# Four-batch products of v_m and w1: two heads side by side on the row halves of the array, three terms of 64 rows each

## The chip, the core and the metric

The kernel runs on one core of a Trainium2 chip. The metric is the time of one execution on the device in microseconds (us); several executions are timed and the median counts, and one execution is recorded by the profiler. The engines are called PE (the matrix engine; PEld is its loading of weights), DVE (VectorE), ACT (ScalarE), POOL (GpSimd) and SP (SyncE, which here only issues transfers).

## The reference

Eight batches of eight heads with 576 rows of 64 pass through an attention over 32 memories per head, and the result through four experts.

```python
a = softmax(phi)                                  # b h s m
k_m = np.einsum('bhsm,bhsd->bhmd', a, k)
v_m = np.einsum('bhsm,bhsd->bhmd', a, v)
attn = softmax(scale * np.matmul(q, k_m.transpose(0, 1, 3, 2)))
x = np.matmul(attn, v_m)                          # 4608 x 512 once the heads are joined
for e in range(E):                                # 4 experts
    h = np.maximum(x @ w1[e], 0.0)                # w1: 512 x 1024
    out += p[:, e:e + 1] * (h @ w2[e])            # w2: 1024 x 512
```

## The kernel before

**Precision.** A factor stands as a high part rounded to float32r and a low part, the remainder, and a product is made of terms: high by high, high by low, low by high.

**What is multiplied.** `x` is never formed. The kernel multiplies v_m by w1 first and attn by that: `h = relu(attn @ (v_m @ w1))`. `v_m @ w1` for a batch, an expert and a half `fh` of the 1024 columns is a tile `vw`. It is made in one of two ways. `vw_mm` (lines 539 to 545) does it for two heads and two batches at a time. `four_mm` does it for one head and four batches at a time (4 x 32 memories fill the 128 columns of weights). The second way serves expert 3 of the batches 0 to 3 and all experts of the batches 4 to 7, in all 5 pairs of expert and batch group, times two halves, times eight heads: 80 products.

**How a four-batch product is laid.** `write_v` (434 to 450) puts v_m of four batches into the tile `vs`: the 64 partitions 0 to 63 hold the high part of a head, the partitions 64 to 127 its low part. The 64 rows of w1 that belong to the head come doubled over both halves from an input `w1d` made for this. So two matmuls of 128 rows and 512 columns give all four terms, with the high part of w1 (`w[:, 0]`) and then with the low (`w[:, 1]`).

**Its steps.** `units_four` (601 to 618) makes the work of a pair `hp` of heads. A load takes a staged 512 KB tile of `w1d`; `four_split` makes the high part on ACT (line 163) and the low part on POOL (line 164), once for each of the two heads; `four_mm` fills a PSUM bank; `four_out` (590 to 595) copies it out, the high part on ACT (592) and the low part on DVE (593), and gives the bank back; `to_memory` (572 to 576) has POOL store the result, to be loaded by `load_vw`.

**What sets the order.** From step 36 on the order is written by hand: `plan[s]` holds what is issued in step s, in the order of the calls of `at`. Up to step 191 (`BEGIN` is 192) a step is a `first` (attn by vw, lines 649 to 651) and a `second` (h by w2, lines 682 to 684), with four banks of the pool "pm" between `first`, the products and the attention. From there on `unit(u)` runs, four steps long, with products by `product` (line 1019), `rows` (933 to 935) and, in every fourth unit, `middle` (1057 to 1059). In it "pm" has two banks, for the four-batch products, for `middle` and for the attention (scores, line 463, and transposes, line 521). Banks go round in turn: `bank` takes the one that was given back first, and an instruction that writes a bank waits for the last one that read it. 16 of the 80 products lie before step 192, 64 in units.

A unit issues on PE, in this order: `run_plan(s)`, six matmuls "a11", six `rows`, `run_plan(s + 1)` behind which `middle` stands, "a12", six `rows`, "t2", `run_plan(s + 2)`, "t3", six `rows`, "t1", `run_plan(s + 3)`, "n4", six `rows`, "a22". `add_in` (1037, DVE) adds each result to the accumulator. `x_relu` (967, ACT) and `x_out` (975, 976, 979 and in part 947 and 948) prepare the next unit. DVE, ACT and POOL each work their instructions in order, so an instruction that `run_plan` puts in stands behind all that the unit has issued there.

With the profile's line numbers:

Of the kernel before, what the change touches and what calls it, by code (L numbers as in the profile page):

```python
# [9 lines left out]
F32 = mybir.dt.float32  # L10
F32R = mybir.dt.float32r
# [17 lines left out]
PAIR = E * STEPS  # L29
# [9 lines left out]
FOUR = (3, 0)  # L39

FOUR_AT = ((6, 8, 10, 13), (15, 17, 20, 22))
FOUR_LAG = 2


W2_AT = (20, 23, 25, 27)
# [7 lines left out]
ATT = {  # L53
    2: (22, 30, 48, (92, 96, 101), (111, 112, 113)),
    3: (38, 46, 65, (116, 118, 120), (PAIR + 2, PAIR + 4, PAIR + 6)),
    4: (88, 96, 114, (PAIR + 75, PAIR + 79, PAIR + 91), (PAIR + 99, PAIR + 103, PAIR + 107)),
    5: (107, PAIR - 2, PAIR + 16, (PAIR + 111, PAIR + 115, PAIR + 123), (PAIR + 119, PAIR + 125, PAIR + 131)),
    6: (PAIR + 3, PAIR + 14, PAIR + 32, (2 * PAIR + 23, 2 * PAIR + 27, 2 * PAIR + 35), (2 * PAIR + 31, 2 * PAIR + 33, 2 * PAIR + 43)),
    7: (PAIR + 18, PAIR + 32, PAIR + 50, (2 * PAIR + 98, 2 * PAIR + 102, 2 * PAIR + 106), (2 * PAIR + 115, 2 * PAIR + 116, 2 * PAIR + 117)),
}  # L60

# [7 lines left out]
BEGIN = SEVEN[0] * PAIR + SEVEN[1] * STEPS  # L69
# [9 lines left out]
FOUR_AT_7 = ((0, 4, 8, 12), (16, 20, 24, 28))  # L79
# [3 lines left out]


@with_exitstack
def body(ctx: ExitStack, tc: tile.TileContext, qm, qt, kv, kvt, phi, prob, w1, w1d, w2, out):
    nc = tc.nc
    pool = lambda name, **k: ctx.enter_context(tc.tile_pool(name=name, bufs=1, **k))
    const, wp, work, att = pool("const"), pool("wp"), pool("work"), pool("att")
# [5 lines left out]
    def bank(tag, *shape):  # L95
        n = idle[tag].popleft()
        out = banks[:, n, :]
        m = 1
        for d in shape:
            m *= d  # L100
        names = "abcd"[:len(shape)]
        out = out[:, :m].rearrange(
            f"p ({' '.join(names)}) -> p {' '.join(names)}", **dict(zip(names, shape))
        )
        lent[id(out)] = tag, n, out
        return out

    def give(ps):
        tag, n, _ = lent.pop(id(ps))
        idle[tag].append(n)  # L110
# [12 lines left out]

    def source(key):
        kind, *i = key
        return {"kv": kv, "kvt": kvt, "qm": qm, "qt": qt, "w1": w1, "w1d": w1d, "w2": w2}[kind][tuple(i)]

    order, staged, count, spare = [], {}, [0, 0], []

# [32 lines left out]
    def split(dst, raw, eng):  # L162
        nc.scalar.copy(dst[:, 0, :], raw)  # L163
        eng.tensor_sub(dst[:, 1, :], raw, dst[:, 0, :].bitcast(F32))  # L164
# [6 lines left out]
    def unit_w1(k, e, fh, g):  # L171
        def emit(raw):
            for i in range(2):
                split_w1(raw, fh, 2 * g + i, nc.vector)
        return ("w1", e, fh, g), emit
# [79 lines left out]
    st = {}  # L255
# [157 lines left out]
    def slot(b, h):  # L413
        return h ^ TURN[b % 4]
# [19 lines left out]
    def write_v(b, pair):  # L434


        if b % 4 == 0:
            st["vs", b // 4] = att.tile([P, 2, 4, P], F32R, name="vs", tag="vs")
        vs = st["vs", b // 4]
        vt = vts[b // 2].rearrange("p (g a) s c -> p g a s c", g=2) if pair else None  # L440
        v = st["vh", b].rearrange("p s (g a) m -> p s g a m", g=2)
        for h in range(4):
            q = slot(b, h)
            rq, c = slice(64 * (q % 2), 64 * (q % 2) + 64), slice(M * q, M * q + M)
            rh = slice(64 * (h % 2), 64 * (h % 2) + 64)
            for i in range(2):
                src = v[rq, i, :, q // 2, :].bitcast(F32)
                nc.sync.dma_start(vs[64 * i:64 * i + 64, :, h, c].bitcast(F32), src)
                if pair:
                    nc.sync.dma_start(vt[rh, :, h // 2, i, c].bitcast(F32), src)  # L450

    def tiles(t0):
        return (2, P) if t0 < 4 else (1, 64)
# [118 lines left out]
    def to_memory():  # L572
        for key, t in done:
            vwd[key] = dram.tile([P, 2, 512], F32, name="vwd" + "".join(map(str, key)))
            nc.gpsimd.dma_start(vwd[key], t.bitcast(F32))
        done.clear()

    def four_split(raw, i):
        w = wp.tile([P, 2, 512], F32R, name="w1", tag="w1", bufs=4)
        split(w, raw[:, i, :], nc.gpsimd)  # L580
        return w

    def four_mm(n, h, w):
        g, vs = h // 4, st["vs", n]
        ps = bank("pm", 512)
        for a in range(2):
            nc.tensor.matmul(ps, vs[:, g, h % 4, :], w[:, a, :], start=a == 0, stop=a == 1)  # L587
        return ps

    def four_out(n, e, fh, h, ps):  # L590
        t = att.tile([P, 2, 512], F32R, name="vst", tag="kvs", bufs=KVS)
        nc.scalar.copy(t[:, 0, :], ps)
        nc.vector.tensor_sub(t[:, 1, :], ps, t[:, 0, :].bitcast(F32))
        give(ps)
        done.append(((n, e, fh, h // 4, h % 4), t))

    def four(n, e, fh, h, w):
        to_memory()
        four_out(n, e, fh, h, four_mm(n, h, w))

    def units_four(n, e, fh, hp, gap=1):

        kept = {}
        def load(raw):
            kept["raw"] = raw
            kept[0] = four_split(raw, 0)
        def other():
            kept[1] = four_split(kept["raw"], 1)
        out = [(0, (("w1d", e, fh, hp), load)), (gap, other)]
        for i in range(2):  # L610
            h, x = 2 * hp + i, FOUR_LAG + gap * i
            if gap == 1:
                out.append((x, lambda i=i, h=h: four(n, e, fh, h, kept[i])))
                continue
            out.append((x, lambda i=i, h=h: kept.update({2 + i: four_mm(n, h, kept[i])})))
            out.append((x + 1, lambda i=i, h=h: four_out(n, e, fh, h, kept[2 + i])))
            out.append((x + 2, to_memory))
        return out

    def load_vw(k, e, odd, fh):  # L620
        b = 2 * k + odd
# [90 lines left out]
    def at(s, unit):  # L712
        plan[s].append(unit if isinstance(unit, tuple) else (None, unit))
# [80 lines left out]
    for k in range(NG):  # L794
        for e in range(E):
            s = k * PAIR + e * STEPS
            nk, ne = (k, e + 1) if e + 1 < E else (k + 1, 0)
            if nk == NG:
                continue
            by_four = ne >= FOUR[nk // 2]  # L800
            if s == 0:
                for j2 in range(4):
                    at(s + W2_AT[j2], unit_w2(nk, ne, j2))
                for fh in range(2):
                    for g in range(2):
                        at(s + W1_AT[2 * fh + g], unit_w1(nk, ne, fh, g))
                        for i in range(2):
                            vw_at(s + VW_AT + 4 * fh + 2 * g + i, nk, ne, fh, 2 * g + i, (0, 1))
                continue
            for j2 in range(4 if nk == 0 else 0):  # L810
                for i, u in enumerate(units_w2(nk, ne, j2)):
                    at(s + W2_FROM + 2 * j2 + i, u)
            for j in range(NJ if nk and s + STEPS < BEGIN else 0):
                at(s + W2_AGAIN + j, lambda a=(nk, ne, j): load_w2(*a))
            for fh in range(2):
                when, gap = (FOUR_AT_7, 2) if s >= BEGIN else (FOUR_AT, 1)
                for hp in range(NP if by_four and nk % 2 == 0 else 0):
                    for i, u in units_four(nk // 2, ne, fh, hp, gap):
                        at(s + when[fh][hp] + i, u)
                if by_four and nk % 2 == 0 and gap == 1:  # L820
                    at(s + when[fh][NP - 1] + FOUR_LAG + 2, to_memory)
                for odd in range(2 if by_four else 0):
                    when = VW_LOAD_AT if s < BEGIN else VW_LOAD_7
                    at(s + when[odd][fh], lambda a=(nk, ne, odd, fh): load_vw(*a))
                for g in range(0 if by_four else 2):
                    last = s + STEPS == BEGIN
                    when = (LAST_PAIR_AT if last else PAIR_AT)[fh]
                    for i, u in enumerate(units_w1(ne, fh, g)):
                        at(s + PAIR_W1[fh][2 * g + i], u)
                        gap = 1 if last and fh and g else 0  # L830
                        vw_steps(s + when[2 * g + i] + i * gap, gap, nk, ne, fh, 2 * g + i, (0, 1))
# [33 lines left out]
    for block in range(UNITS // 4):  # L865
        _, e, fh, _, _ = place_of(4 * block)
# [272 lines left out]
    with tc.manual_schedule():  # L1139
        raw = {key: take(later) for later, key in enumerate(early)}  # L1140
# [153 lines left out]
```

## Time and profile before

| what | value |
|---|---|
| median of 3 runs | 1377.34 us (1377.04 to 1381.64) |
| the profiled execution | 1377.26 us, of it 1375.5 us span |
| PE, DVE, ACT, POOL busy | 98%, 63%, 47%, 51% of the span |
| granted clock of PE | 0.998 |
| four-batch matmuls (line 587) | 160, from 257.2 to 1012.6 us |
| loads of `w1d` | 40 of 512 KB, 6.3 us to landing |

How it is read: PE records carry the start of an instruction; their ends are modelled, and matmuls overlap in the records. What a matmul costs in a stream is therefore the distance between the start of one and the start of the next, not its length. In a row of the timeline stand the start, the length, engine, line, operation, tiles, shape and count, and in brackets the idle time ahead of it.

### The profile page before, as it was taken

What the parts mean: (1) busy time and instruction counts of PE and PEld (TensorE: products, weight loads), DVE (VectorE), ACT (ScalarE), POOL (GpSimd) and SP (SyncE); (2) the same over time, 40 slices, a digit from 0 to 9 for tenths busy, and PEclk for the clock granted to TensorE, in tenths of its full rate; (3) what the DMA queues carried; (4) which work ended last, traced back from release to release, by engine and by line L of the source; (5) the groups of instructions that cost most, each with busy time, mean ns of one, the idle gap of its engine ahead of it and who ended that gap; (6) DMA issues with size and microseconds to landing.
All of it is one profiled execution on the core that took longest, in us unless ns stands there. A gap on an engine that the chain in (4) does not pass through costs nothing.

```text
span 1375.5 us, 26069 instructions
## 1 busy us (share of the span) xinstructions
PE 1353.9 (98%) x9182; PEld 1257.8 (91%) x9182; DVE 859.9 (63%) x1966; ACT 644.8 (47%) x1552; POOL 695.7 (51%) x743
## 2 busy tenths in 40 slices
PE   7899999999999999999999999999999999999998
PEld 6788888888888888889999999999999999999998
DVE  7875644445556445456677767767667666666665
ACT  6664565445535655453454544555543333333332
POOL 4300383648533626446866676677754334334432
PEclk9999999999999999999999999999999999999999
DMA  7652373898666454465789998999984866666661
GB/s 258 232 184 78 132 250 124 284 305 277 227 228 245 133 195 158 155 236 212 250 260 316 364 331 301 310 313 335 328 281 130 263 177 183 180 180 175 172 177 72
DMA packets 104338, 309.82 MB, mean 225 GB/s; under 512 B 25232, under 2 KB 26384, under 8 KB 104208
## 3 DMA queue, kind: packets, MB, share of 16 engines
q1 hardware_dynamic: 83472, 232.65, 53.6%
q0 software_dynamic: 19584, 71.31, 13.3%
q10 hardware_dynamic: 1152, 4.19, 0.8%
q8 instruction: 73, 1.20, 0.4%
q14 instruction: 57, 0.47, 0.1%
HBM read 221.85 MB, written 84.93 MB: 223 GB/s over the span
## 4 chain that ended last, share of the span: by engine, by line
PE 90%; DVE 4%; DMA 2%; ACT 1%; issue 1%; POOL 1%; SPq 0%; ACTq 0%; POOLq 0%; DVEq 0%
PE banks L1019 28%; PE banks L684 7%; PE banks L683 7%; PE banks L682 7%; PE banks L933 6%; PE banks L934 6%; PE banks L935 6%; PE banks L649 4%; PE banks L650 3%; PE banks L651 3%; PE banks L587 2%; PE banks L463 2%; PE banks L357 2%; PE banks L1057 1%; PE banks L1058 1%; PE banks L1059 1%
## 5 line engine op out<-in xcount | busy, mean ns | idle before, releaser
L1037 DVE SCALAR_TENSOR_TENSOR acc<-banks,pt,acc 128x256 f32<-128x256 f32 x528 | 253.0, 479 | 137.1 <-PE banks L1019 131.1
L164 POOL TENSOR_TENSOR w<-stage,w 128x512 fp32r<-128x512 f32 x134 | 173.8, 1298 | 149.0 <-ACT w L163 141.6
L1019 PE MATMUL banks<-w,a 128*128 128x256 f32 x1344 | 192.3, 282 | 0.3 <-DVE acc L1037 0.2
L933 PE MATMUL banks<-AT,vw 128*128 128x256 f32 (+1 forms) x640 | 189.5, 296 | 0.0
L934 PE MATMUL banks<-AT,vw 128*128 128x256 f32 (+1 forms) x640 | 188.9, 295 | 0.0
L935 PE MATMUL banks<-AT,vw 128*128 128x256 f32 (+1 forms) x640 | 188.8, 295 | 0.0
L1019 PEld LDWEIGHTS banks<-w,a 128*128 128x128 f32 x1344 | 179.2, 189 | 5.7 <-issue 0.6
L1000 POOL TENSOR_TENSOR vt<-ph,vt 128x512 fp32r<-128x512 f32 x80 | 103.8, 1297 | 108.2 <-ACT vt L999 71.8
L663 DVE SCALAR_TENSOR_TENSOR h<-banks,h 128x256 fp32r<-128x256 f32 x192 | 80.3, 420 | 124.0 <-ACT h L661 81.9
L684 PE MATMUL banks<-w,h 128*128 128x512 f32 x384 | 150.6, 393 | 2.2 <-DVE h L663 2.2
L682 PE MATMUL banks<-w,h 128*128 128x512 f32 x384 | 151.6, 395 | 0.1
L683 PE MATMUL banks<-w,h 128*128 128x512 f32 x384 | 151.1, 393 | 0.0
L661 ACT ACTIVATE h<-banks 128x256 fp32r<-128x256 f32 x192 | 73.4, 384 | 125.1 <-PE banks L651 99.6
L985 ACT ACTIVATE a<-banks 128x512 fp32r<-128x512 f32 x80 | 47.9, 598 | 166.1 <-DVE ph L991 131.1
L1010 POOL TENSOR_TENSOR tl<-xs,tl 128x256 fp32r<-128x256 f32 x80 | 59.3, 742 | 131.0 <-ACT tl L1009 72.2
L934 PEld LDWEIGHTS banks<-AT,vw 128*128 128x128 f32 x640 | 120.7, 189 | 0.1
L933 PEld LDWEIGHTS banks<-AT,vw 128*128 128x128 f32 x640 | 120.4, 188 | 0.4
L935 PEld LDWEIGHTS banks<-AT,vw 128*128 128x128 f32 x640 | 120.3, 188 | 0.0
L649 PE MATMUL banks<-AT,vw 128*128 128x320 f32 (+1 forms) x384 | 117.5, 307 | 1.3 <-DVE vw L563 0.9
L346 POOL TENSOR_TENSOR kvs<-stage,kvs 128x512 fp32r<-128x512 f32 x58 | 76.2, 1334 | 81.7 <-ACT kvs L345 73.7
L650 PE MATMUL banks<-AT,vw 128*128 128x320 f32 (+1 forms) x384 | 113.6, 296 | 0.0
L1019 PE MATMUL banks<-w,vt 128*128 128x256 f32 x768 | 112.6, 280 | 0.2 <-DVE acc L1037 0.2
(155 smaller groups left out, 3153.5 us busy)
## 6 DMA issues: line engine op xcount, KB each, us to landing
w<-kw SPq DMA_DIRECT2D x92, 512.0 KB, 5.7
vwd<-vst POOLq DMA_DIRECT2D x80, 512.0 KB, 6.5
vw<-vwd SPq DMA_DIRECT2D x320, 128.0 KB, 6.0
w<-v SPq DMA_DIRECT2D x68, 512.0 KB, 5.9
stage<-in_w SPq DMA_DIRECT2D x44, 512.0 KB, 4.4
stage<-in_w1d SPq DMA_DIRECT2D x40, 512.0 KB, 6.3
stage<-in_kv SPq DMA_DIRECT2D x32, 512.0 KB, 4.7
kw<-w POOLq DMA_DIRECT2D x24, 512.0 KB, 5.5
```

The source lines that it names most:

```text
L164: eng.tensor_sub(dst[:, 1, :], raw, dst[:, 0, :].bitcast(F32))
L649: nc.tensor.matmul(ps, w[:, 0, f], at_t[:, g, 0, c], start=g == 0, stop=False)
L650: nc.tensor.matmul(ps, w[:, 0, f], at_t[:, g, 1, c], start=False, stop=False)
L682: nc.tensor.matmul(po[t], x[:, 0, :], w[:, 0, :], start=j == 0, stop=False)
L683: nc.tensor.matmul(po[t], x[:, 0, :], w[:, 1, :], start=False, stop=False)
L684: nc.tensor.matmul(po[t], x[:, 1, :], w[:, 0, :], start=False, stop=j == NJ - 1)
L933: nc.tensor.matmul(ps, w[:, 0, f], at_t[:, g, 0, c], start=g == 0, stop=False)
L934: nc.tensor.matmul(ps, w[:, 0, f], at_t[:, g, 1, c], start=False, stop=False)
L935: nc.tensor.matmul(ps, w[:, 1, f], at_t[:, g, 0, c], start=False, stop=g == 1)
L1000: GP.tensor_sub(D[:, 1], d, D[:, 0].bitcast(F32))
L1019: nc.tensor.matmul(ps, a[:, l, jj], w[:, r, c], start=start and jj + i == 0, stop=jj == 1 and i == 2, skip_group_check=True,)
L1037: VE.scalar_tensor_tensor(a, src, p, a, ALU.mult, ALU.add)
```

## The change

Both heads of a pair are multiplied together. `vs` now has the layout of the tile that `vw_mm` uses: head 2hp on partitions 0 to 63, head 2hp + 1 on partitions 64 to 127, high and low part beside each other. A tile of w1 as it stands in the ordinary input `w1` has the rows of both heads on the same halves. So `w1d` goes, a load and a split serve two heads (20 loads and 40 splits instead of 40 and 80), and a pair takes six matmuls of 64 rows by 512 columns, alternating between the two halves and writing two banks, instead of four of 128 rows. The term low by low is left out.

The plan moves with it. In units, the second tile's split is now four steps behind the load; both heads are multiplied three steps behind their tile's split, always in `run_plan(s + 3)` of a unit, and take both banks; they are copied out in `run_plan(s)` and `run_plan(s + 1)` of the next unit. Before, the head products stood in `run_plan(s)` and `run_plan(s + 2)`, and were copied out one step later each. The attention's scores and transposes that fell on `run_plan(s + 3)` of these units are moved to `run_plan(s)`, where a bank is given back. Before step 192 both heads of a pair are multiplied in one step instead of in two, and copied out in that step and the next.

```diff
-FOUR_LAG = 2
+FOUR_LAG, FOUR_LAG_7 = (2, 2), (3, 4)
...
-    4: (88, 96, 114, (PAIR + 75, PAIR + 79, PAIR + 91), (PAIR + 99, PAIR + 103, PAIR + 107)),
...
+    4: (88, 96, 114, (PAIR + 75, PAIR + 79, PAIR + 91), (PAIR + 100, PAIR + 104, PAIR + 108)),
...
-            st["vs", b // 4] = att.tile([P, 2, 4, P], F32R, name="vs", tag="vs")
-        vs = st["vs", b // 4]
+            st["vs", b // 4] = att.tile([P, NP, 2, P], F32R, name="vs", tag="vs")
+        vs = st["vs", b // 4].rearrange("p (g a) s c -> p g a s c", g=2)
...
-                nc.sync.dma_start(vs[64 * i:64 * i + 64, :, h, c].bitcast(F32), src)
-                if pair:
-                    nc.sync.dma_start(vt[rh, :, h // 2, i, c].bitcast(F32), src)
+                for t in [vs] + [vt] * pair:
+                    nc.sync.dma_start(t[rh, :, h // 2, i, c].bitcast(F32), src)
...
-    def four_mm(n, h, w):
-        g, vs = h // 4, st["vs", n]
-        ps = bank("pm", 512)
-        for a in range(2):
-            nc.tensor.matmul(ps, vs[:, g, h % 4, :], w[:, a, :], start=a == 0, stop=a == 1)
+    def four_mm(n, hp, w):
+
+        vs, ps = st["vs", n], [bank("pm", 512) for _ in range(2)]
+        for t, (l, r) in enumerate(((0, 0), (0, 1), (1, 0))):
+            for i in range(2):
+                half = slice(64 * i, 64 * i + 64)
+                nc.tensor.matmul(
+                    ps[i], vs[half, hp, l, :], w[half, r, :], start=t == 0, stop=t == 2
+                )
         return ps
...
+    def units_four(n, e, fh, g, when, lag):
 
         kept = {}
         def load(raw):
             kept["raw"] = raw
+            kept["w", 0] = four_split(raw, 0)
+        def out(i, hp):
+            to_memory()
+            four_out(n, e, fh, 2 * hp + i, kept["ps", hp][i])
+        units = []
+        for a in range(2):
+            x, hp = when[2 * g + a], 2 * g + a
+            if a:
+                units.append((x, lambda: kept.update({("w", 1): four_split(kept["raw"], 1)})))
+            else:
+                units.append((x, (("w1", e, fh, g), load)))
+            units.append((x + lag[0], lambda a=a, hp=hp: kept.update({("ps", hp): four_mm(n, hp, kept["w", a])})))
+            for i in range(2):
+                units.append((x + lag[1] + i, lambda i=i, hp=hp: out(i, hp)))
+            units.append((x + lag[1] + 2, to_memory))
+        return units
```

Three places show the new order, all around the first transposes of batch 4 among the units. The first is PE in `run_plan(s + 3)`, between "t1" and "n4". Before (L1019 with `t_` is "t1", with `tl` "n4"; L521 are the transposes):

```order
L1019 MATMUL banks<-w_6160,t_7104 128x256 x2
L1019 MATMUL banks<-w_6281,t_7104 128x256 [waits DMAHW7_49]
L1019 MATMUL banks<-w_6281,t_7104 128x256 x2
L521 MATMUL banks<-ident,at 128x128 x4
L1019 MATMUL banks<-w_6257,tl 128x256 [waits DVE_49]
L1019 MATMUL banks<-w_6257,tl 128x256 x2
L1019 MATMUL banks<-w_6279,tl 128x256 x3
L933 MATMUL banks<-AT,vw 128x320
L934 MATMUL banks<-AT,vw 128x320
```

The same place with the change (L588 is the four-batch product):

```order
L1019 MATMUL banks<-w_6144,t_7088 128x256 x2
L1019 MATMUL banks<-w_6265,t_7088 128x256 [waits DMAHW3_49]
L1019 MATMUL banks<-w_6265,t_7088 128x256 x2
L588 MATMUL banks<-w_7175,vs 128x512 x2
L588 MATMUL banks<-w_7175,vs 128x512 [waits Pool_49]
L588 MATMUL banks<-w_7175,vs 128x512 x3
L1019 MATMUL banks<-w_6241,tl 128x256 [waits DVE_49]
L1019 MATMUL banks<-w_6241,tl 128x256 x2
L1019 MATMUL banks<-w_6263,tl 128x256 x3
L933 MATMUL banks<-AT,vw 128x320
```

The product of two heads, six matmuls of 64 rows, stands where the transposes stood.

The second place is PE one step later, in `run_plan(s)` of the next unit, between "a22" (L1019 with `a`) and "a11" (with `a_7208`). Before (L587 is the product of one head):

```order
L1019 MATMUL banks<-w_6160,a 128x256 [waits DVE_49]
L1019 MATMUL banks<-w_6160,a 128x256 x2
L1019 MATMUL banks<-w_6281,a 128x256 x3
L587 MATMUL banks<-w_7240,vs 128x512 [waits DVE_49]
L587 MATMUL banks<-w_7240,vs 128x512 [waits Pool_49]
L1019 MATMUL banks<-w_6131,a_7208 128x256 [waits DVE_49]
L1019 MATMUL banks<-w_6131,a_7208 128x256 x2
L1019 MATMUL banks<-w_6224,a_7208 128x256 x3
L933 MATMUL banks<-AT,vw 128x320 [waits DVE_49]
```

The same place with the change (L520 are the transposes; "a11" is `a_7192`):

```order
L1019 MATMUL banks<-w_6144,a 128x256 [waits DVE_49]
L1019 MATMUL banks<-w_6144,a 128x256 x2
L1019 MATMUL banks<-w_6265,a 128x256 x3
L520 MATMUL banks<-ident,at 128x128 [waits DVE_49]
L520 MATMUL banks<-ident,at 128x128 x3
L1019 MATMUL banks<-w_6115,a_7192 128x256 [waits Activation_49]
L1019 MATMUL banks<-w_6115,a_7192 128x256
L1019 MATMUL banks<-w_6115,a_7192 128x256 [waits Pool_49]
L1019 MATMUL banks<-w_6208,a_7192 128x256 x3
L933 MATMUL banks<-AT,vw 128x320
```

The product has gone, and the transposes stand right behind "a22" with a wait for DVE, which they did not have.

The third place is DVE over the same stretch, from the `add_in` behind "n4" on. Before (L1037 is `add_in`, L1007 the copy for the next "n4", L593 a copy out of a product, L533 that of the transposes):

```order
L1037 SCALAR_TENSOR_TENSOR acc<-banks,pt,acc 128x256 [waits PE_49]
L1007 SCALAR_TENSOR_TENSOR xs<-banks,ph 128x256 [waits Pool_49]
L948 SCALAR_TENSOR_TENSOR hm<-banks,hm 128x2x64 [waits Activation_49]
L1037 SCALAR_TENSOR_TENSOR acc<-banks,pt,acc 128x256 [waits PE_49]
L533 TENSOR_TENSOR AT<-banks,AT 128x2x256 [waits DMASW7_49,DMASW5_49,DMAHW0_49,DMASW3_49,DMAHW7_49,DMASW1_49,Activation_49]
L1037 SCALAR_TENSOR_TENSOR acc<-banks,pt,acc 128x256 [waits PE_49]
L975 SCALAR_TENSOR_TENSOR ph<-banks,ph 128x256 [waits Activation_49,Pool_49]
L948 SCALAR_TENSOR_TENSOR hm<-banks,hm 128x2x64 [waits Activation_49]
L593 TENSOR_TENSOR vst<-banks,vst 128x512 [waits DMASW6_49,DMASW4_49,Activation_49]
L1037 SCALAR_TENSOR_TENSOR acc<-banks,pt,acc 128x256 [waits DVE_49,PE_49]
```

DVE with the change (L596 is the copy out of a product, L532 that of the transposes):

```order
L1037 SCALAR_TENSOR_TENSOR acc<-banks,pt,acc 128x256 [waits PE_49]
L1007 SCALAR_TENSOR_TENSOR xs<-banks,ph 128x256 [waits Pool_49]
L948 SCALAR_TENSOR_TENSOR hm<-banks,hm 128x2x64 [waits Activation_49]
L1037 SCALAR_TENSOR_TENSOR acc<-banks,pt,acc 128x256 [waits PE_49]
L596 TENSOR_TENSOR vst<-banks,vst 128x512 [waits DMASW4_49,DMASW2_49,Activation_49]
L1037 SCALAR_TENSOR_TENSOR acc<-banks,pt,acc 128x256 [waits PE_49]
L975 SCALAR_TENSOR_TENSOR ph<-banks,ph 128x256 [waits Activation_49,Pool_49]
L948 SCALAR_TENSOR_TENSOR hm<-banks,hm 128x2x64 [waits Activation_49]
L596 TENSOR_TENSOR vst<-banks,vst 128x512 [waits DMASW6_49,DMASW4_49,Activation_49]
L532 TENSOR_TENSOR AT<-banks,AT 128x2x256 [waits DMASW7_49,DMASW5_49,DMAHW3_49,DMASW3_49,DMAHW4_49,DMASW1_49,Activation_49]
L1037 SCALAR_TENSOR_TENSOR acc<-banks,pt,acc 128x256 [waits DVE_49,PE_49]
```

The copy out of the first head stands between the `add_in` behind "a22" and that behind "a11"; the copy out of the transposes has moved behind the copy out of the second head, ahead of the `add_in` behind "a12".

More of the change, by code (lines that the diff above doesn't have):

```diff
@@ L55 @@
     3: (38, 46, 65, (116, 118, 120), (PAIR + 2, PAIR + 4, PAIR + 6)),
-    4: (88, 96, 114, (PAIR + 75, PAIR + 79, PAIR + 91), (PAIR + 99, PAIR + 103, PAIR + 107)),
-    5: (107, PAIR - 2, PAIR + 16, (PAIR + 111, PAIR + 115, PAIR + 123), (PAIR + 119, PAIR + 125, PAIR + 131)),
-    6: (PAIR + 3, PAIR + 14, PAIR + 32, (2 * PAIR + 23, 2 * PAIR + 27, 2 * PAIR + 35), (2 * PAIR + 31, 2 * PAIR + 33, 2 * PAIR + 43)),
+    4: (88, 96, 114, (PAIR + 75, PAIR + 79, PAIR + 91), (PAIR + 100, PAIR + 104, PAIR + 108)),
+    5: (107, PAIR - 2, PAIR + 16, (PAIR + 112, PAIR + 116, PAIR + 124), (PAIR + 120, PAIR + 125, PAIR + 132)),
+    6: (PAIR + 3, PAIR + 14, PAIR + 32, (2 * PAIR + 24, 2 * PAIR + 28, 2 * PAIR + 36), (2 * PAIR + 32, 2 * PAIR + 33, 2 * PAIR + 44)),
     7: (PAIR + 18, PAIR + 32, PAIR + 50, (2 * PAIR + 98, 2 * PAIR + 102, 2 * PAIR + 106), (2 * PAIR + 115, 2 * PAIR + 116, 2 * PAIR + 117)),
@@ L85, in body @@
 @with_exitstack
-def body(ctx: ExitStack, tc: tile.TileContext, qm, qt, kv, kvt, phi, prob, w1, w1d, w2, out):
+def body(ctx: ExitStack, tc: tile.TileContext, qm, qt, kv, kvt, phi, prob, w1, w2, out):
     nc = tc.nc
@@ L125, in source @@
         kind, *i = key
-        return {"kv": kv, "kvt": kvt, "qm": qm, "qt": qt, "w1": w1, "w1d": w1d, "w2": w2}[kind][tuple(i)]
+        return {"kv": kv, "kvt": kvt, "qm": qm, "qt": qt, "w1": w1, "w2": w2}[kind][tuple(i)]
     order, staged, count, spare = [], {}, [0, 0], []
@@ L576, in to_memory, with four_split @@
         done.clear()
-    def four_split(raw, i):
+    def four_split(raw, hp):
         w = wp.tile([P, 2, 512], F32R, name="w1", tag="w1", bufs=4)
-        split(w, raw[:, i, :], nc.gpsimd)
+        split(w, raw[:, hp % 2, :], nc.gpsimd)
         return w
-    def four_mm(n, h, w):
-        g, vs = h // 4, st["vs", n]
-        ps = bank("pm", 512)
-        for a in range(2):
-            nc.tensor.matmul(ps, vs[:, g, h % 4, :], w[:, a, :], start=a == 0, stop=a == 1)
+    def four_mm(n, hp, w):
[6 more added lines that the diff above has]
+                )
         return ps
@@ L595, in four_out @@
         done.append(((n, e, fh, h // 4, h % 4), t))
[L597 to L601, printed above, removed]
+    def units_four(n, e, fh, g, when, lag):
         kept = {}
@@ L605, in load @@
             kept["raw"] = raw
[L606 to L618, printed above, removed]
+            kept["w", 0] = four_split(raw, 0)
[14 more added lines that the diff above has]
+        return units
     def load_vw(k, e, odd, fh):
@@ L815, in body @@
             for fh in range(2):
[L816 to L821, printed above, removed]
+                when, lag = (FOUR_AT_7, FOUR_LAG_7) if s >= BEGIN else (FOUR_AT, FOUR_LAG)
+                for g in range(2 if by_four and nk % 2 == 0 else 0):
+                    for i, u in units_four(nk // 2, ne, fh, g, when[fh], lag):
+                        at(s + i, u)
                 for odd in range(2 if by_four else 0):
@@ L1278 @@
         "w1": c(moe_w1.reshape(E, 2, 2, P, 2, 512).transpose(0, 4, 1, 3, 2, 5)),
-        "w1d": c(
-            np.tile(moe_w1.reshape(E, NP, 2, D, 2, 512).transpose(0, 4, 1, 3, 2, 5), (1, 1, 1, 2, 1, 1))
-        ),
         "w2": c(moe_w2.reshape(E, NJ // 2, 2, P, DM).transpose(0, 1, 3, 2, 4)),
```

## The prediction

> **What bounds the kernel now.** I read the busy table first, then the chain that ended last, then PE's waits, and last the table of stretches over the units that hold 64 of the 80 products.
>
> ```profile
> PE 1353.9 (98%) x9182; PEld 1257.8 (91%) x9182; DVE 859.9 (63%) x1966; ACT 644.8 (47%) x1552; POOL 695.7 (51%) x743
> PE 90%; DVE 4%; DMA 2%; ACT 1%; issue 1%; POOL 1%; SPq 0%; ACTq 0%; POOLq 0%; DVEq 0%
> PE banks L1019 <- DVE acc L1037: 1.3, 4, 0.4
> 610.00:1020.00 410.00, 408.69 (x3083) 394.31 (x3082) 288.40 (x657) 198.33 (x439) 287.83 (x323) 1.00 0.88 298
> ```
>
> PE is the bound: 98% busy, 90% of the chain. In the stretch from 610 to 1020 us (columns: length, busy time of PE, PEld, DVE, ACT, POOL, clock, DMA) it is busy for 408.69 of 410 us, and its waits for `add_in` come to 1.3 us in the whole run (third line: total, times, longest). So whatever ACT, POOL and the transfers are spared buys nearly nothing, and every 0.1 us added on PE or in a wait of PE is added to the end. A step's rhythm is read from one unit with no attention in it, first PE, then DVE, then ACT:
>
> ```profile
> 924.33 0.87 PE L1019 MATMUL banks<-w,a 128*128 128x256 f32 x6
> 925.04 0.64 PE L587 MATMUL banks<-w,vs 128*128 128x512 f32 x2
> 925.52 0.88 PE L1019 MATMUL banks<-w,a 128*128 128x256 f32 x6
> 926.23 0.28 PE L933 MATMUL banks<-AT,vw 128*128 128x256 f32 x1
> 926.94 0.88 PE L1019 MATMUL banks<-w,a 128*128 128x256 f32 x6
> 927.65 0.28 PE L933 MATMUL banks<-AT,vw 128*128 128x256 f32 x1
> 928.37 0.51 PE L1019 MATMUL banks<-vw,vt 128*128 128x256 f32 x3
> 929.06 0.62 PE L587 MATMUL banks<-w,vs 128*128 128x512 f32 x2
> 929.52 0.52 PE L1019 MATMUL banks<-vw,vt 128*128 128x256 f32 x3
> ...
> 924.50 0.41 DVE L1007 SCALAR_TENSOR_TENSOR xs<-banks,ph 128x256 f32<-128x256 f32 x1
> 925.24 0.48 DVE L1037 SCALAR_TENSOR_TENSOR acc<-banks,pt,acc 128x256 f32<-128x256 f32 x1 [0.34 <-PE banks L1019]
> 926.43 0.48 DVE L1037 SCALAR_TENSOR_TENSOR acc<-banks,pt,acc 128x256 f32<-128x256 f32 x1 [0.70 <-PE banks L1019]
> 926.83 0.41 DVE L975 SCALAR_TENSOR_TENSOR ph<-banks,ph 128x256 f32<-128x256 f32 x1
> 928.21 0.69 DVE L593 TENSOR_TENSOR vst<-banks,vst 128x512 fp32r<-128x512 f32 x1 [0.96 <-ACT vst L592]
> 928.81 0.48 DVE L1037 SCALAR_TENSOR_TENSOR acc<-banks,pt,acc 128x256 f32<-128x256 f32 x1
> ...
> 924.94 0.41 ACT L1009 CAST tl<-xs 128x256 fp32r<-128x256 f32 x1 [3.19 <-DVE xs L1007]
> 925.25 0.61 ACT L163 CAST w<-stage 128x512 fp32r<-128x512 f32 x1
> 925.77 0.59 ACT L967 ACTIVATE ph<-banks 128x512 f32<-128x512 f32 x1
> 926.40 0.41 ACT L976 CAST a<-ph 128x256 fp32r<-128x256 f32 x1
> 927.28 0.41 ACT L979 CAST t<-ph 128x256 fp32r<-128x256 f32 x1 [0.47 <-DVE ph L975]
> 927.59 0.58 ACT L592 CAST vst<-banks 128x512 fp32r<-128x512 f32 x1
> ```
>
> PE's rows are "a22", a product, "a11", `rows`, "a12", `rows`, "t2", a product, "t3". A product (two matmuls of 512 columns) takes 0.48 and 0.46 us from its start to the next start, so 0.235 us a matmul.
>
> **The products themselves.** A pair of heads takes 4 x 0.235 = 0.94 us now. With the change six matmuls run in two lanes. What leaving the full array costs stands in the trace, where the last transposes of a batch use 64 rows:
>
> ```profile
> 373.78 0.39 PE L683 MATMUL banks<-w,hm 128*128 128x512 f32 x1
> 374.01 0.39 PE L684 MATMUL banks<-w,hm 128*128 128x512 f32 x1
> 374.32 0.33 PE L521 MATMUL banks<-ident,at 64*128 64x64 f32 x2
> 374.68 0.42 PE L649 MATMUL banks<-AT,vw 128*128 128x320 f32 x1
> 374.93 0.31 PE L650 MATMUL banks<-AT,vw 128*128 128x320 f32 x1
> 375.08 0.31 PE L651 MATMUL banks<-AT,vw 128*128 128x320 f32 x1
> ...
> 373.78 0.19 PEld L684 LDWEIGHTS banks<-w,hm 128*128 128x128 f32 x1
> 374.32 0.20 PEld L521 LDWEIGHTS banks<-ident,at 64*128 64x128 f32 x2 [0.35 <-issue]
> 374.67 0.19 PEld L649 LDWEIGHTS banks<-AT,vw 128*128 128x128 f32 x1 [0.15 <-DVE h L663]
> 374.78 0.19 PEld L650 LDWEIGHTS banks<-AT,vw 128*128 128x128 f32 x1
> ```
>
> Between matmuls of one shape the next weights load while the last matmul streams (L684's load at 373.78 is beside L683). Into the 64-row shape they do not: the load of L521 begins at 374.32, 0.31 us after L684 where 0.23 is usual, and out of it L649's load stands open, so that L650 is 0.25 behind L649 instead of 0.15. A change of shape thus costs 0.08 or 0.09 for the array to run empty and 0.10 for an uncovered load, 0.19 us, twice a pair: 0.38. Inside, a load holds PE 0.11 us (374.67 to 374.78): six loads in a row start six matmuls 0.11 apart, the last ends 0.235 after its start, 5 x 0.11 + 0.235 = 0.79; two lanes of 3 x 0.235 = 0.71 fit beneath. A pair takes 0.79 + 0.38 = 1.17 us, 0.23 more than now, and 40 pairs **+9 us**. No row shows two halves at work together. The bounds: 0.71 and no edges, -0.23 a pair, -9 us; one after the other, 6 x 0.235 + 0.38 = 1.79, +0.85 a pair, +34 us. I take the middle, as loads beside a matmul are in every row.
>
> If the array ran empty at each turn between the halves as well, five more edges would cost 5 x 0.19 a pair, +38 us on 40. No row shows such a turn. The Trainium skill, "TensorEngine Tiling (Array Packing)", section "Key Properties", has the array drained by a change of the tiling mode, not of the tile alone; the rows agree on the change of mode (0.08 us), and by it there are two edges a pair and not seven.
>
> **The bank that attention waits for.** In units, one product now takes both banks. The first comes free in `run_plan(s)`, when DVE has copied the first head out, and there the order sets the attention's matmul, ahead of "a11". In DVE's queue the copy stands behind the `add_in` of "a22", which can start only when "a22" has ended: the row at 925.24, 0.20 us after PE's next start at 925.04. `add_in` holds DVE 0.40 (926.43 to 926.83), the copy takes 0.69: 1.29 us after PE could have gone on. ACT's half of the copy follows L1009 (924.94 + 0.31 + 0.58 = 925.83) and pushes DVE's to 925.83 + 0.69, 1.48 us. With the uncovered load, 1.5 us of a standing PE, where before at least the six "n4", six `rows` and six "a22" lay between. This falls on the steps 228, 232, 236, 240, 244, 248, 252, 260, 280, 284, 288, 292 and 300: 13 x 1.5 = **+20 us**. Behind the waiting instruction stands all of PE. Bounds 1.3 and 1.7 a time, +17 to +22 us.
>
> On five further occasions (`middle` in 233, 249 and 281, transposes in 253 and 289) the instruction gets the second head's bank in `run_plan(s + 1)`. From the end of "a11" (926.23) the queue runs through `add_in`, L975, L979, the copy on ACT and that on DVE, to 928.21 + 0.69 = 928.90, 2.67 us; PE has six `rows`, 0.71, to fill it. 2.0 + 0.1 uncovered load, 5 x 2.1 = **+10 us**; bounds 1.2 (should the ACT part run ahead) and 2.5, +6 to +12.
>
> **"t3" loses its cover.** "t3" overwrites the bank that the `add_in` of "a12" reads. That `add_in` ends at 928.81 + 0.48 = 929.29, and PE came to "t3" at 929.52 only because a product lay ahead of it from 929.06. With the products gone from there, and from ahead of "a11", PE is at "t3" 0.23 us too early even on the old chain. On the new one the first head's copy is put in ahead of everything: 0.58 on ACT ahead of L967, 0.69 on DVE, which moves L975 by up to 0.5. In attention units its outputs come in too, behind the second head's copy:
>
> ```profile
> L473 DVE TENSOR_REDUCE mx<-banks x24: 353/680/693, 22.5 to 1044.2; 128x16 f32<-128x512 f32 x16, 64x8 f32<-64x256 f32 x8
> L476 DVE TENSOR_TENSOR at<-banks,mx x24: 354/691/692, 23.2 to 1044.6; 128x512 f32<-128x512 f32 x16, 64x256 f32<-64x256 f32 x8
> L533 DVE TENSOR_TENSOR AT<-banks,AT x24: 278/686/692, 31.9 to 1068.8; 128x512 fp32r<-128x512 f32 x16, 128x128 fp32r<-128x128 f32 x8
> ```
>
> That is 0.69 or 1.37 us. Units with `middle` (six matmuls of 512 columns, 6 x 0.23 = 1.38 us of PE, twice) or with a wait in `run_plan(s + 1)` are late enough; 22 of 32 are not. The bounds are nothing (`rows` of 320 columns give PE 6 x 0.03 more) and 0.8 in each, 0 to +18 us. I take half, 0.4: **+9 us**, since this is a difference of two chains of nearly one length.
>
> **What costs nothing.** 40 splits and 20 loads go: POOL's share of a split is 1.29 us, but PE's 1.3 us of waiting leave nothing to gain, and I count at most -2 us.
>
> ```profile
> L164 POOL TENSOR_TENSOR w<-stage,w x134: 1264/1290/1749, 18.2 to 1009.6; 128x512 fp32r<-128x512 f32 x134
> ```
>
> SP's queue is held longer at two steps (240, 280), where a staged load waits for a tile whose second split is four steps off; behind it are loads of `vw` needed ten steps later. The three buffers of the copies are each written again about a unit (9 us) after POOL has issued their store. The copies of the first eight pairs, before step 192, have four banks and a step of PE between; if that cover failed, it would be 8 x 0.3, +2 us.
>
> **The sum**, on the profiled execution of 1377.26 us (1375.5 us span and 1.8 around it; the median of the runs, 1377.34, is the same): 9 + 20 + 10 + 9 = +48, so **1425 us**, 3.5% slower.
>
> **The rivals.**
> - *One half after the other*: array and banks serve one half at a time, so that two heads at once is only written and not done. +34 instead of +9: 1450 us. For it speaks that no row shows two halves at once; against it, nothing but that the two use different rows and banks. 0.13.
> - *A load waits for the matmul of its own half*: three rounds of 0.11 + 0.235 and the second half's start 0.11 later are 1.15 inside instead of 0.79, 0.36 x 40 = +14 more, 1439 us. Against it L684's load, which runs beside L683 on the same rows. 0.08. The Trainium skill, "TensorE: Matmul & The Clock Gate", section "The mechanism", has this rule (weights load beside a running matmul only where the row groups differ); for the full array the trace differs, for halves no run here shows it.
> - *The waits are covered*: ACT and DVE, relieved of splits and with longer products in `run_plan(s + 3)`, are ahead by enough. Then only the products count: 1386 us, up to 1398 if a third of the waits stay. Against it: each of the 13 begins with the end of "a22", which no lead shortens. 0.12.
> - *Faster*: both halves in step and weights of the half shape loaded beneath the full one. -9 us, 1368 us. It decides where the two edges of a pair cost under 0.23 us together, and it needs the waits to be covered as well. Against it 0.38 us at 374 us. 0.04.
>
> The forecast has the rest, 0.63, and its own range is 1404 to 1440 us. For 8 in 10 I leave out the faster case, most of the covered one and the upper half of the first: 1394 to 1452 us. A measurement of this kernel can tell 0.5%, about 7 us, from no change: faster 0.04, same 0.03 (low ends of the covered case), slower 0.93.
>
> **What would show it.** The six matmuls of a product about 0.11 us apart and some 1.17 us from its first start to that of "n4", less what shows ahead of it; steps of 0.23 would be the first rival. PE's waits for DVE, 1.3 us now, at some 40: 13 of 1.5 at the attention's lines and 5 of 2 at `middle` and the transposes, all named after the copy's line, and shorter ones at line 1019 after `add_in`. DVE's and ACT's busy time hardly moves, POOL's falls by 40 x 1.29 = 52 us. The forecast is wrong where PE's waits stay under 10 us, or where the product takes less than 0.94.

## The result and the profile after

| | before | after |
|---|---|---|
| median | 1377.19 us (1376.64 to 1381.64) | 1431.44 us (1429.2 to 1432.64) |
| ratio | | 1.0389, 95% interval 1.0377 to 1.0402 |
| profiled execution, its span | 1377.26, 1375.5 us | 1432.54, 1430.7 us |

The changed kernel is 3.9% slower. The difference of the two spans, 55.2 us, is what has to be accounted for. First the page of after (busy us, share of the span, instructions; then the chain that ended last), and the same table of stretches as before, over the units that hold 32 of the 40 pairs (length, busy time and count of PE, PEld, DVE, ACT and POOL, clock, share of DMA, GB/s):

```profile
PE 1374.9 (96%) x9262; PEld 1256.7 (88%) x9262; DVE 864.5 (60%) x1966; ACT 624.2 (44%) x1512; POOL 644.7 (45%) x703
PE 84%; DVE 6%; DMA 4%; ACT 3%; issue 2%; POOL 1%; SPq 0%; DVEq 0%; ACTq 0%; POOLq 0%
600.00:1080.00 480.00, 444.63 (x3254) 411.14 (x3253) 303.41 (x679) 188.52 (x423) 251.83 (x297) 0.99 0.74 247
```

PE was busy for 408.69 of 410 us in such a stretch and now stands for 35.4 of 480. POOL lost 51.0 us of work, ACT 20.6. None of it shows at the end: full_array_copy_early below has the same relief (POOL 644.1 us) without the halves and the late copies, and is not faster than before. What PE waits for (total us, times, longest), the four costliest of the units:

```profile
PE banks L520 <- DVE vst L596: 12.6, 9, 1.9
PE banks L1019 <- DVE acc L1037: 10.8, 23, 1.4
PE banks L462 <- DVE vst L596: 7.2, 6, 1.3
PE banks L1057 <- DVE vst L596: 5.0, 3, 1.8
```

These are 35.6 us, all new but 1.3. L462 and L520 are the attention, L1057 is `middle`, and all three wait for line 596, the low half of the copy that gives the product's bank back. L1019 after `add_in` (L1037) is "t3" in 21 of the 23 cases.

One of the 13 waits in `run_plan(s)`, in the timeline (start, length, engine, line, operation; in brackets the idle time ahead and what ended it):

```profile
695.13 0.87 PE L1019 MATMUL banks<-w,a 128*128 128x256 f32 x6
695.47 0.40 ACT L1009 CAST tl<-xs 128x256 fp32r<-128x256 f32 x1
695.77 0.59 ACT L595 CAST vst<-banks 128x512 fp32r<-128x512 f32 x1
696.04 0.48 DVE L1037 SCALAR_TENSOR_TENSOR acc<-banks,pt,acc 128x256 f32<-128x256 f32 x1
696.44 0.68 DVE L596 TENSOR_TENSOR vst<-banks,vst 128x512 fp32r<-128x512 f32 x1
697.18 0.66 PE L520 MATMUL banks<-ident,at 128*128 128x128 f32 x4 [1.18 <-DVE vst L596]
```

"a22" starts at 695.13, and six of 256 columns take 0.71 us: PE could go on at 695.84. The `add_in` of "a22" holds DVE from 696.04 to 696.44, the copy to 697.12, and the transposes start at 697.18: 1.34 us. This is the chain of the prediction, row by row.

Now one product, and ahead of it "t1", behind it "n4" and `rows`:

```profile
938.53 0.87 PE L1019 MATMUL banks<-w,t 128*128 128x256 f32 x6
939.33 0.97 PE L588 MATMUL banks<-w,vs 64*128 64x512 f32 x6
940.22 0.98 PE L1019 MATMUL banks<-w,tl 128*128 128x256 f32 x6
941.04 0.31 PE L933 MATMUL banks<-AT,vw 128*128 128x320 f32 x1
```

From first start to next start the product takes 0.89 us. The six of 256 columns ahead take 0.80 and those behind 0.82, where 0.71 was usual (925.52 to 926.23 before): 0.09 and 0.11 for the two changes of shape. So a pair costs 0.89 + 0.20 = 1.09 us, against 0.94. The median over all 40 is 0.155 more than before, 40 x 0.155 = 6.2 us.

How the six lie inside is read from the records of one line in short stretches (count, lengths in ns, first and last start, shapes). The three rows end at 939.5, 939.8 and 940.0 us:

```profile
L588 PE MATMUL banks<-w,vs x2: 495/498/500, 939.3 to 939.3; 64*128 64x512 f32 x2
L588 PE MATMUL banks<-w,vs x4: 388/443/500, 939.3 to 939.7; 64*128 64x512 f32 x4
L588 PE MATMUL banks<-w,vs x6: 388/393/500, 939.3 to 939.9; 64*128 64x512 f32 x6
```

They come in pairs. Of the records' starts, the second of a pair lies 3 ns behind the first, and the pairs at 0, 0.34 and 0.57 us: a round of two matmuls costs 0.232 us, the first one 0.107 more for its uncovered load. The two halves' loads start together as well.

A "t3" (the last row) that waits:

```profile
742.65 0.69 DVE L596 TENSOR_TENSOR vst<-banks,vst 128x512 fp32r<-128x512 f32 x1 [0.49 <-ACT vst L595]
...
743.26 0.68 DVE L472 TENSOR_REDUCE mx<-banks 128x16 f32<-128x512 f32 x1
743.35 0.52 PE L1019 MATMUL banks<-vw,vt 128*128 128x256 f32 x3
743.97 0.69 DVE L475 TENSOR_TENSOR at<-banks,mx 128x512 f32<-128x512 f32 x1
744.58 0.48 DVE L1037 SCALAR_TENSOR_TENSOR acc<-banks,pt,acc 128x256 f32<-128x256 f32 x1
...
745.11 0.61 PE L1019 MATMUL banks<-w,vt 128*128 128x256 f32 x3 [1.24 <-DVE acc L1037]
```

The second head's copy and the attention's two outputs keep DVE from 742.65 to 744.58; only then does the `add_in` of "a12" run that frees "t3"'s bank. There are 21 such waits of 0.32 to 1.59 us (measured between starts), 13.5 us in all.

One thing the prediction did not have. Ahead of a `middle` PE stood for 1.85 us, and soon after it ran at half clock (timeline, then the stretches from 711 to 714 and from 714 to 717.5; the number after the five engines is the granted clock):

```profile
713.13 0.50 PE L1057 MATMUL banks<-w,hm 128*128 128x512 f32 x1 [1.85 <-DVE vst L596]
713.47 0.39 PE L1058 MATMUL banks<-w,hm 128*128 128x512 f32 x1
713.69 0.42 PE L1059 MATMUL banks<-w,hm 128*128 128x512 f32 x1
713.92 0.62 PE L1057 MATMUL banks<-w,hm 128*128 128x512 f32 x1
714.34 0.63 PE L1058 MATMUL banks<-w,hm 128*128 128x512 f32 x1
714.77 0.63 PE L1059 MATMUL banks<-w,hm 128*128 128x512 f32 x1
...
711.00:714.00 3.00, 1.15 (x7) 0.83 (x6) 1.72 (x4) 1.38 (x3) 1.75 (x4) 0.99 0.09 35
714.00:717.50 3.50, 3.50 (x16) 3.21 (x15) 0.48 (x1) 0.00 (x0) 0.03 (x1) 0.52 0.66 269
```

The same matmul of 512 columns follows the one ahead after 0.22 us, and from 713.92 on after 0.42 or 0.43. That lasts 3.4 us and happens four times in this execution (from 713.9, 771.9, 789.0 and 864.1 us), with 5.4 us more between the starts of the matmuls in them.

The account, from the starts of PE's records: products 6.2; the 13 waits in `run_plan(s)` 18; those of `middle` and two transposes in `run_plan(s + 1)` 9.7; "t3" 13.5; half clock 5.4. Together 52.8 of the 55.2 us.

### The profile page after: what moved, and what is told of

Same layout as the page of the kernel before. It is cut to its first block, busy times and chain, and to the rows that moved or that the text cites. A ratio compares the mean times of both kernels' runs of the same rounds, so it can differ in the third digit from the quotient of the medians.

```text
span 1430.7 us, 25999 instructions
## 1 busy us (share of the span) xinstructions
PE 1374.9 (96%) x9262; PEld 1256.7 (88%) x9262; DVE 864.5 (60%) x1966; ACT 624.2 (44%) x1512; POOL 644.7 (45%) x703
## 4 chain that ended last, share of the span: by engine, by line
PE 84%; DVE 6%; DMA 4%; ACT 3%; issue 2%; POOL 1%; SPq 0%; DVEq 0%; ACTq 0%; POOLq 0%
PE banks L1019 26%; PE banks L686 6%; PE banks L685 6%; PE banks L684 6%; PE banks L933 5%; PE banks L935 5%; PE banks L934 5%; PE banks L651 3%; PE banks L652 3%; PE banks L653 3%; PE banks L588 2%; PE banks L462 2%; PE banks L357 2%; PE banks L1057 1%; PE banks L1058 1%
## 5 line engine op out<-in xcount | busy, mean ns | idle before, releaser
L1037 DVE SCALAR_TENSOR_TENSOR acc<-banks,pt,acc 128x256 f32<-128x256 f32 x528 | 253.7, 481 | 189.3 <-PE banks L1019 183.4
L1019 PE MATMUL banks<-w,a 128*128 128x256 f32 x1344 | 192.3, 285 | 0.3 <-DVE acc L1037 0.2
L1019 PEld LDWEIGHTS banks<-w,a 128*128 128x128 f32 x1344 | 177.5, 190 | 3.2 <-issue 0.6
L164 POOL TENSOR_TENSOR w<-stage,w 128x512 fp32r<-128x512 f32 x94 | 121.8, 1298 | 108.9 <-ACT w L163 107.1
L1019 PE MATMUL banks<-w,vt 128*128 128x256 f32 x768 | 114.8, 284 | 8.4 <-DVE acc L1037 8.4
L1019 PEld LDWEIGHTS banks<-w,vt 128*128 128x128 f32 x768 | 102.7, 190 | 13.0 <-DVE acc L1037 11.6
```

What stands on the lines that cost most here:

```text
L1019: nc.tensor.matmul(ps, a[:, l, jj], w[:, r, c], start=start and jj + i == 0, stop=jj == 1 and i == 2, skip_group_check=True,)
L1037: VE.scalar_tensor_tensor(a, src, p, a, ALU.mult, ALU.add)
```

## The experiments

Three ideas stood against the account above, which is the prediction's (A: the order of the copies costs most, the halves little). B: the 64-row matmuls cost the greater part. C: the copies set the pace of DVE and ACT wherever they stand, so that waits only move. D, which no expectation names: the attention's move to `run_plan(s)` does not matter by itself, the waits would come anyway with one product for two banks. The first four ran on one chip, where the kernel before took 1378.14 us; the last three on one where it took 1378.91.

**full_array.** The plan of after, with four matmuls of 128 rows a pair instead of six of 64. Each sums over both heads, so a bank holds the sum of two heads' products of high by high and high by low.

```diff
-        for t, (l, r) in enumerate(((0, 0), (0, 1), (1, 0))):
-            for i in range(2):
-                half = slice(64 * i, 64 * i + 64)
+        for i in range(2):
+            for r in range(2):
                 nc.tensor.matmul(
-                    ps[i], vs[half, hp, l, :], w[half, r, :], start=t == 0, stop=t == 2
+                    ps[i], vs[:, hp, i, :], w[:, r, :], start=r == 0, stop=r == 1
```

> The changed kernel's plan, loads, splits and banks, but each product is again four matmuls of the whole array, two into each bank, with the tiles as they are now laid: each bank then sums over the rows of both heads, so the products are not those of the reference. Theory A (the time went into waits of PE that the plan made: for a bank that DVE has not yet copied out, and at t3; the halves themselves cost 0.15 us a pair, 6 us): the waits stay and only the 6 us go, 1425 us (1422 to 1428). Theory B (the time went into the halves: 64-row matmuls, the edges into and out of them and what follows on PE): back to 1378 to 1385 us.

Measured 1424.65 us, ratio 1.0338 (1.0324 to 1.0352): 6.8 us less than after. PE's waits are the same, a line number lower:

```profile
PE banks L520 <- DVE vst L595: 12.6, 9, 1.9
PE banks L1018 <- DVE acc L1036: 10.8, 22, 1.5
PE banks L462 <- DVE vst L595: 7.2, 6, 1.3
PE banks L1056 <- DVE vst L595: 5.0, 3, 1.8
```

With the matmuls of before the kernel is still 46.5 us slower than before. B falls.

**copy_early.** In units the first head is copied out in the step of its product, `run_plan(s + 3)`, and the second in `run_plan(s)`, instead of one step later each.

```diff
-FOUR_LAG, FOUR_LAG_7 = (2, 2), (3, 4)
+FOUR_LAG, FOUR_LAG_7 = (2, 2), (3, 3)
```

> The changed kernel with one number changed: in units the first head is copied out in run_plan(s + 3), right behind the product, and the second in run_plan(s), a step earlier each. Theory A: a bank is free at run_plan(s) and another at run_plan(s + 1), so the 18 waits for a bank go (28 us) and with them the lowered clock behind the longest (5 us); t3 keeps waits only in units with attention (10 times 0.5, 5 us). 1377 + 6 + 5 = 1388 us (1384 to 1396). Theory B: the products are untouched, 1425 to 1432 us. Theory C (the copies set the pace on DVE and ACT wherever they stand, so that waits only move): 1415 to 1431 us.

Measured 1388.61 us, ratio 1.0082 (1.0068 to 1.0096): one number gives back 42.8 us. The place of 697.18 above, and what is left of the four lines of PE's waits:

```profile
692.54 0.59 ACT L595 CAST vst<-banks 128x512 fp32r<-128x512 f32 x1 [1.92 <-PE banks L588]
693.16 0.69 DVE L596 TENSOR_TENSOR vst<-banks,vst 128x512 fp32r<-128x512 f32 x1 [1.03 <-ACT vst L595]
...
694.15 0.87 PE L1019 MATMUL banks<-w,a 128*128 128x256 f32 x6
694.85 0.60 PE L520 MATMUL banks<-ident,at 128*128 128x128 f32 x4
...
PE banks L1019 <- DVE acc L1037: 0.9, 3, 0.4
...
PE banks L1057 <- DVE vst L596: 0.2, 1, 0.2
```

The copy now ends at 693.85, beside "n4" and `rows`, and the transposes follow "a22" after 0.70 us. C falls: the waits went and did not move. "t3" waits 3 times instead of 21, 0.28, 0.22 and 0.25 us, 0.76 in all between starts (the three waits of 0.9 us that the list has at L1019 are one of "n4" and two of "a11"). So its waits too came from the copies that stood ahead of it in DVE's and ACT's queues: the missing cover alone, which this kernel has as well, costs at most those 0.76 us. That the time falls on the expected 1388 us is in part luck: "t3" kept 0.76 us and not 5, while the halves cost 8 and not 6 and a wait of 2.5 us came new (next run).

**full_array_copy_early.** Both edits, with the same sum over two heads.

> Both edits together: copies a step earlier, and each product as four matmuls of the whole array (each bank sums over both heads, so the products are not those of the reference). Theory A: 6 us below the one with the halves, 1382 us (1378 to 1390). Theory B: 1376 to 1380 us, with 45 us or more between this and the one with the halves.

Measured 1380.61 us, ratio 1.0023 (1.0014 to 1.0031). The halves cost 1388.61 - 1380.61 = 8.0 us with the early copy and 6.8 without, so the two parts of the change add up. What is left is 2.5 us over before; its list of PE's waits has one that before lacks, and that copy_early has too:

```profile
PE banks L520 <- POOL at L495: 2.4, 1, 2.4
```

It is in step 289. In batch 6 the change puts the scores one step later (from step 287 to 288) and leaves the first transposes in 289, so the transposes wait for their own softmax. In after, the bank's wait at the same place covers it. No run moved these transposes alone.

**attention_later.** The copies as in after; 10 of the 13 matmuls of the attention that stood in `run_plan(s)` are moved to a later step (nine by one step, the transposes of step 300 by five), and the transposes of step 289 to 301; the other three of the 13 stay.

```diff
-    4: (88, 96, 114, (PAIR + 75, PAIR + 79, PAIR + 91), (PAIR + 100, PAIR + 104, PAIR + 108)),
+    4: (88, 96, 114, (PAIR + 75, PAIR + 79, PAIR + 91), (PAIR + 101, PAIR + 104, PAIR + 109)),
...
-    6: (PAIR + 3, PAIR + 14, PAIR + 32, (2 * PAIR + 24, 2 * PAIR + 28, 2 * PAIR + 36), (2 * PAIR + 32, 2 * PAIR + 33, 2 * PAIR + 44)),
+    6: (PAIR + 3, PAIR + 14, PAIR + 32, (2 * PAIR + 24, 2 * PAIR + 29, 2 * PAIR + 37), (2 * PAIR + 33, 2 * PAIR + 45, 2 * PAIR + 49)),
```

> The changed kernel, but the attention's scores and transposes of units without middle stand in run_plan(s + 1) (10 of the 13; the three in units with middle stay), and two transposes of batch 6 later still. Theory A: at run_plan(s + 1) the first bank has just been copied out, so 10 waits of 1.35 us go, and their outputs no longer stand ahead of the add_in that t3 waits for, some 6 us: 1410 us (1405 to 1417). The waits at middle stay at 2 us each. Theory B: 1429 to 1433 us, as nothing of the products changes.

Measured 1409.63 us, ratio 1.0228 (1.0214 to 1.0242): 21.8 us less than after. What is left of the waits at the attention's lines:

```profile
PE banks L520 <- DVE vst L596: 2.7, 2, 1.4
PE banks L462 <- DVE vst L596: 1.3, 1, 1.3
```

These three are the matmuls of the steps 232, 248 and 280, which stayed (1.45 to 1.54 us between starts); the ten that moved wait no more for the copy, which is 13.6 us. `middle` keeps its own waits (5.5) and L1019 keeps 6.7. The rest of the 21.8 us is not only "t3": the two waits of transposes in `run_plan(s + 1)` for the copy have gone, one stretch at half clock is left of four, and a new wait of 1.7 us (L520, for line 980 on POOL) counts against them. Each product takes both banks here as well, so the wait comes from the place of the matmul against the copy, and not from the number of banks alone: D falls.

**heads_apart.** From here on the plan of copy_early is the base. The three terms of the first head are issued ahead of the three of the second.

```diff
-        for t, (l, r) in enumerate(((0, 0), (0, 1), (1, 0))):
-            for i in range(2):
-                half = slice(64 * i, 64 * i + 64)
+        for i in range(2):
+            half = slice(64 * i, 64 * i + 64)
+            for t, (l, r) in enumerate(((0, 0), (0, 1), (1, 0))):
```

> The plan of copy_early (1388.61 us), with the six matmuls of a pair in another order: the three terms of the first head, then the three of the second, instead of alternating between the halves. If the halves work side by side only where a matmul on one half is issued right behind one on the other (issue in order, one matmul waiting on each half), just one of the five steps inside overlaps: 5 x 0.232 us instead of the 3 x 0.232 that the trace of the changed kernel shows, so 2 x 0.232 = 0.46 more on each of 40 pairs, +18.6 us: 1407 us (1402 to 1411). If each half takes its three whatever the order: 1388.6 us (1386 to 1392). If the turn from one half to the other had a price of its own, which alternating pays five times and this order once, it would be faster than 1388.

Measured 1390.23 us, ratio 1.0085 (1.0070 to 1.0100) against copy_early's 1.0082. The records of a pair, in stretches that end at 903.4, 903.7 and 904.0 us:

```profile
L588 PE MATMUL banks<-w,vs x2: 498/498/498, 903.2 to 903.2; 64*128 64x512 f32 x2
L588 PE MATMUL banks<-w,vs x4: 393/446/498, 903.2 to 903.6; 64*128 64x512 f32 x4
L588 PE MATMUL banks<-w,vs x6: 393/393/498, 903.2 to 903.8; 64*128 64x512 f32 x6
```

Pairs again, now 10 ns apart instead of 3. The records do not name the half. But two of the six carry the signal that ends a head: in the order of issue they are the third and the sixth, and by their starts the fifth and the sixth (34 of 40 pairs). So the fourth matmul in the order starts 10 ns behind the first and some 0.33 us ahead of the second: each half runs its own three, alternating is not needed, and a turn between the halves has no price that shows.

**fourth_term.** The term low by low is added, eight matmuls of 64 rows a pair.

```diff
-        for t, (l, r) in enumerate(((0, 0), (0, 1), (1, 0))):
+        for t, (l, r) in enumerate(((0, 0), (0, 1), (1, 0), (1, 1))):
...
-                    ps[i], vs[half, hp, l, :], w[half, r, :], start=t == 0, stop=t == 2
+                    ps[i], vs[half, hp, l, :], w[half, r, :], start=t == 0, stop=t == 3
```

> The plan of copy_early (1388.61 us) with the term low by low put in again: eight matmuls of 64 rows a pair instead of six. If the two halves work at the same time, a round of two costs 0.232 us: 40 x 0.232 = +9.3, 1398 us (1396 to 1400). If the halves shared a port or the array and only appeared together in the records, a round costs 0.46: +18.6, 1407 us. With loads 0.11 us apart as the prediction had it, 2 x 0.11 = 0.22 a pair, which this run does not tell from the first; the starts in its trace do (pairs 0.23 apart, or six 0.11 apart).

Measured 1398.07 us, ratio 1.0141 (1.0124 to 1.0158). The difference of the ratios, 0.0059, is 8.1 us, and between the starts in its trace a pair takes 1.13 us instead of 0.90, 40 x 0.23 = 9.2. Two more matmuls cost one round: the halves do work at the same time.

**edges_doubled.** The middle round is one matmul of 128 rows, which sums the term high by low over both heads into the first head's bank, so the array changes its shape four times a pair.

```diff
+            if t == 1:
+                nc.tensor.matmul(ps[0], vs[:, hp, l, :], w[:, r, :], start=False, stop=False)
+                continue
             for i in range(2):
```

> The plan of copy_early (1388.61 us). The middle round of a pair (high by low on both halves) is replaced by one matmul of 128 rows, which sums that term over both heads into the first bank; the streaming stays 3 x 0.23 us, but the array changes its shape four times a pair instead of twice. If the price of the halves is the two changes of shape (0.09 to run empty and 0.105 for an uncovered load, each), two more cost 0.39 on each of 40 pairs: +15.6, 1404 us (1399 to 1408). If the price lies in the 64-row matmuls themselves, a third of them is gone here and the time falls below 1388.6, to about 1386.

Measured 1406.19 us, ratio 1.0199 (1.0184 to 1.0215): 0.0117 above copy_early, 16.1 us, 0.40 a pair.

```profile
903.50 0.49 PE L591 MATMUL banks<-w,vs 64*128 64x512 f32 x2
903.93 0.50 PE L587 MATMUL banks<-w,vs 128*128 128x512 f32 x1
904.36 0.50 PE L591 MATMUL banks<-w,vs 64*128 64x512 f32 x2
904.80 0.97 PE L1022 MATMUL banks<-w,tl 128*128 128x256 f32 x6
```

Each of the three takes 0.43 or 0.44 us where a round inside one shape takes 0.232: 0.20 at every change of shape. That is the whole price of the halves, two changes a pair.

No run beats the kernel before. Of the plans with the two halves the best is copy_early, 0.8% slower.

## Why the prediction was right, step by step

The forecast of 1425 us was 6.4 us under the median of 1431.44, and its mechanism held. That the sum came so near is in part luck: the products and the two bank terms were 5.1 us too high together, "t3" and the clock 9.9 too low. Term by term:

- **The products**, +9 forecast, 6.2 between the starts, 6.8 and 8.0 by the two pairs of runs. The edges were right: 0.20 each where 0.19 was read at 374 us, and edges_doubled gives 0.20. The step that was off is "six loads in a row start six matmuls 0.11 apart". Loads of the two halves go together, so the inside is three rounds of 0.232, 0.70 us, and not 0.79. The bound "two lanes of 3 x 0.235" was the value to take, with its edges. For the same reason one sign of being wrong came true by its letter: "where the product takes less than 0.94" is met from its first start to the next start (0.89). It was written for the wrong stretch, as 0.09 us of the edges shows ahead of that start and 0.11 behind the next; the whole pair takes 1.09.
- **One half after the other** (1450) is refuted by fourth_term. **A load waits for the matmul of its own half** (1439) is refuted by the trace: three rounds would be 1.15 us inside, and 0.89 was taken, load included. **Faster** (1368) needed two edges under 0.23 us together, and they cost 0.40. The five further edges at the turns between the halves (+38 us) do not show: the rounds follow each other after 0.232 us.
- **The bank, `run_plan(s)`**, 13 x 1.5 = +20 forecast, 18 measured, 1.33 to 1.54 each. The lower bound, 1.3, fits where ACT's half has run ahead, as at 695.77.
- **The bank, `run_plan(s + 1)`**, +10 forecast, 9.7 measured. With the line above 27.7 us; moving 10 of the 13 away returned 21.8, of which 13.6 are those ten and some is "t3" (10.8 to 6.7 us in the waits). These two terms were the core of the forecast.
- **"t3"**, 22 x 0.4 = +9 forecast, 13.5 measured, on 21 occasions. This is the term of the wrong size: 0.64 us each. The ordinary units wait 0.32 to 0.69; four wait 0.86 to 1.59, where DVE still had the attention's outputs to work off (as at 743.26). The prediction named these outputs but took one middle value for all units. Its heading, "loses its cover", was also half wrong: copy_early lacks the same cover and waits 0.76 us, so the late copies made the rest.
- **The waits are covered** (1386): not in after, but copy_early makes that very case and takes 1388.61, of which 6 to 8 us are the halves.
- **Left out altogether**: the clock, 5.4 us. The prediction took 0.998 of before for granted; after was granted 0.993. That the waits bring it is argued, not shown: each of the four half-clock stretches begins within 3.4 us of waits of 1.5 to 2.0 us in all, copy_early, which has lost these waits, has one such stretch in the units, behind the one wait of 2.5 us that it has there, and before has none. But full_array has the same waits and fewer stretches, in after the longest wait of L520, 1.9 us at 896 us, has none behind it, and full_array_copy_early and fourth_term have copy_early's wait (2.4 and 2.5 us) and no such stretch. What decides stays open.
- **What costs nothing**: POOL's 52 us less came as 51.0, and brought nothing, as forecast.

## What to carry to other kernels

- Where one operation now takes every bank of a pool, the price is not in that operation but in whoever asks for a bank next. Follow the release: which engine gives it back, what stands ahead of it in that engine's queue, and how much work the bound engine has until the request. Here a copy one step earlier was worth 42.8 us and the halves of the array 7 to 8.
- Two matmuls of 64 rows, one on each half, took 0.23 us together here (fourth_term), and the price is paid at the edges (0.20 us each here), so the matmuls between two changes of shape must save more than 0.4 us. Three rounds in place of four matmuls saved 0.24.
- When several units wait by one mechanism, size those with extra work in the queue apart from the others.

## What the runs showed of the hardware beyond this

- The two row halves are two streams: their loads and matmuls start 3 ns apart when alternated, and 10 ns apart when one head's three matmuls are all issued ahead of the other's. So a matmul can start ahead of one that was issued before it on the other half.
- A standing PE of 1.5 to 2.0 us out of 3.4 was followed, though not each time, by 3.4 us at half clock, in which matmuls of 512 columns started every 0.42 us instead of 0.23.
